# Linear attention with a gated feed-forward block, fp32: the first and the last instructions are rearranged, and the last four tiles of the normalised input are turned by VectorE by way of DRAM

## The chip, the cores and the metric

One core of one Trainium2 chip. The metric is the device time of one launch in microseconds (us). The core's engines run side by side, each with its own queue of instructions in a fixed order: TensorE (PE in the profile, with its weight loads as PEld), VectorE (DVE), ScalarE (ACT) and GpSimd (POOL) compute, SyncE (SP) issues the DMA transfers. They wait for each other by semaphores.

## The reference

```python
x  = A_x                                  # 1 x 2048 x 512
xn = (x - mean(x)) / sqrt(var(x) + 1e-5)  # over the last axis
q, k, v = (xn @ wqkv) split into 32 heads of 16
pq, pk  = phi(q), phi(k)                  # phi(t) = where(t > 0, t + 1, exp(t)) + 1e-6
kv  = einsum("bhsd,bhse->bhde", pk, v);  z = sum of pk over s
o   = einsum("bhqd,bhde->bhqe", pq, kv) / (einsum("bhqd,bhd->bhq", pq, z) + 1e-6)
s   = o @ wo                              # 512 x 512
g   = silu((gelu(xn @ w_gate) * (xn @ w_up)) @ w_down)   # 512 -> 1792 -> 512
out = x + s * g
```

## The kernel before

All data is fp32. TensorE multiplies in a rounded form (fp32r), so each operand is split in a high part (cast by ScalarE, names ending in h) and a low part (a subtraction by VectorE, names ending in l), and a product is three passes: high by high, high by low, low by high (`three`). The large products are done with seven instead of eight block products (Strassen's way), and X, Y, Z, FX, FY, FZ, dX, dY, dZ are the sums in PSUM that gather them.

*Stages.* The 16 tiles of 128 tokens go in eight pairs n = 0 to 7, each pair with tiles i = 0 and 1. For each pair: load x; `ln` makes the statistics on VectorE, rstd on GpSimd and xn on VectorE (L648); `transp` turns a tile of xn with four 128x128 transposes on TensorE into a PSUM bank pt (L696), from which ScalarE copies it to xt in SBUF (L498); `split_x` casts Xh from pt and VectorE subtracts for Xl; `forms` makes the sums T of xt on GpSimd for the block products; then come the products with the weights of k and q (kq), in X, Y and Z. For pairs 2 to 7 these stand on TensorE as X(n), Y(n), Z(n); for the first two (`CL = 2`) as plain sums k and q. From X, Y and Z come q and k, by ScalarE's kr and qr and VectorE's kp and qp; qp is written to DRAM (q_d) and read back later. `split_xn` splits xn itself (xnh, xnl), and the sums gps gather pk by xn, of four 128-row pieces each. So xn of every tile is read by TensorE's transposes and by `split_xn`.

Meanwhile `prep_early` makes three of the gate and up weights' groups of sums (raw is the load, tmp the sums, we the split result) in four groups each, and writes both halves of each group to DRAM (w_d). From about 133 us on come the feed-forward products with Xh, Xl and the weights w (FX, FY, FZ), the attention's own matrices (pkv, pm, M), then the products with w_down (dX, dY, dZ gathered in acc), and the last sums sps = pq by M (`attn`), in four chunks of 512 tokens by four blocks n of 128 columns. Each sps is multiplied into silu(acc) or a stored g by VectorE (L1323), the transposed x (sxr, loaded by DMA) is added (L504), and the result is stored (`out_tile`).

In `turn`, late in the kernel, a tile q is read back from q_d with its rows mixed (each partition gets the rows of one residue), scaled, and turned by one VectorE transpose in squares of 32x32 (L1260).

*What sets the order.* Every instruction is first recorded by `do` with an engine, a cost, the buffers it reads and writes, and for TensorE a key; a planner (`Plan`) then sets the order on each engine. TensorE follows the list `pe_keys`; the other engines follow from how soon the planner needs a result, with `plan.due` as a time set by hand for some. `KEPT` lists draws that altered this order at random within windows of time, one after the other. Buffers belong to pools of numbered units (`U(name, units, ...)` takes the next free one of its list); the next user of a unit waits for the last reader. A bank is one of the eight in PSUM. `R0`, `R1`, `TMP` are units of 4 KB a partition for raw weights.

```python
    def prep_early(q):
        raw, t = sums_w(q, R0)
        for g, src in enumerate(sources(raw, t)):
            n = GROUPS[g].stop - GROUPS[g].start
            v = raw_tile(R1, f"we{q}{g}", [P, 2, D]) if g % 2 else None
            f = [(half(v, hl) if v else tile_in("up", 34 + hl, [P, D], F32, f"we{q}{g}{hl}")).map(
```

So the groups alternate between two places here: units 34 and 35, and R1.

Of the kernel before, what the change touches and what calls it, by code (L numbers as in the profile page):

```python
# [9 lines left out]
F32 = mybir.dt.float32  # L10
# [5 lines left out]
P = 128  # L16
# [3 lines left out]
    (85, 100, [10000006]),  # L20
    (70, 85, [10000048]),
    (-1, 12, [10000061]),
    (40, 55, [10000175]),
    (135, 200, [10000200]),
    (25, 40, [10000230]),
    (40, 55, [10000342]),
    (85, 100, [10000376]),
    (40, 55, [10000415, 10000462]),
    (500, 560, [10000471]),
    (-1, 12, [10000515]),  # L30
    (500, 560, [10000523, 10000590, 10000640]),
    (115, 135, [10000649]),
    (500, 560, [10000723]),
    (115, 135, [10000785]),
    (500, 560, [10000819, 10000833]),
    (340, 420, [10000924]),
    (115, 135, [10000994]),
    (-1, 12, [10001161, 10001223, 10001300]),
    (270, 340, [10001313, 10001357]),
    (-1, 12, [10001377]),  # L40
    (500, 560, [10001410]),
    (-1, 12, [10001492]),
    (40, 55, [10001818]),
    (-1, 12, [10001854]),
    (500, 560, [10001973]),
    (340, 420, [10002732]),
    (135, 200, [10006848]),
    (85, 100, [10010611]),
    (270, 340, [10010753]),
    (40, 55, [10010839]),  # L50
    (340, 420, [10010858]),
    (500, 560, [10010942, 10011053]),
    (40, 55, [10011765]),
    (135, 200, [10011937]),
    (-1, 12, [1010000092]),
    (340, 420, [1010000637, 1010002072]),
    (25, 40, [1010003933]),
    (500, 560, [1010016325, 1010018040]),
    (70, 85, [1010018047, 1010018667, 1010018893, 1010020523]),
    (55, 70, [1010020607]),  # L60
    (85, 100, [1010021997]),
    (100, 115, [1010030646]),
    (115, 135, [1010032131]),
    (100, 115, [1010033698]),
    (500, 560, [1010034750, 1010034866]),
    (135, 200, [1010038225]),
# [10 lines left out]
WARM = 14, 3  # L77
# [318 lines left out]
def kernel(  # L396
# [78 lines left out]
    q_d = dram_view([NT, KT, P, P], "q_d", NT)  # L475
    g_d = dram_view([D, S // 2], "g_d", NT // 2)
# [86 lines left out]
    idle = bank(0, "warm", (P, P))  # L563
    do("PE", 0.427 * 10, warm, idle, ones, key="warm")
# [59 lines left out]
    CL = 2  # L624
    a21 = [[tile_in("up", 15 + 2 * lo + k, [P, D], F32R, f"a21{lo}{k}") for k in range(2)] for lo in range(2)]
# [8 lines left out]
    def ln(*ts):  # L634
        n = len(ts)
        mv = little("mv", f"mv{ts[0]}", [P, n, 2])
        for i, t in enumerate(ts):
# [7 lines left out]
           rstd, ve, neg_half)  # L645
        for i, t in enumerate(ts):
            xns[t] = U("xn", range(4, 9), f"xn{t}")
            do("DVE", 0.46, lambda o, i, m, r: nc.vector.tensor_scalar(o, i, m, r, op0=ALU.subtract, op1=ALU.mult),  # L648
               xns[t], xs.pop(t), mv[:, i, 0:1], rstd[:, i:i + 1], name=f"xn{t}")
# [38 lines left out]

    def transp(n, i):
        t = tokens[n][i]  # L690

        pt = bank(3 + 2 * n + i if 0 < 2 * n + i < 2 * CL else 1, f"pt{t}", (P, KT, P))

        def run(o, a, b):
            for k in range(KT):
                nc.tensor.transpose(o[:, k, :], a[:, k * P:(k + 1) * P], b)  # L696
            if n == 0 and i == 0:
                warm(idle(), ones(), WARM[1])
        do("PE", 0.4, run, pt, xns[t], ident, key=("T", n, i), name="T", more=(idle,) if n == 0 and i == 0 else ())
# [3 lines left out]
        xts[n, i] = v.part((v.res[i],), (slice(None), i))  # L703
        copy("ACT", xts[n, i], pt, D, f"xt{n}{i}")
        pts[n, i] = pt
# [16 lines left out]
    def split_x(n, i):  # L722
        if i == 0 and n == 0:
            for s in range(2):
                split(xrows("h", s, s + 1, [0]), xrows("l", s, s + 1, [0]), pts[0, 0][:, 2 * s:2 * s + 2], 2 * P, "Xa")
# [13 lines left out]
    def split_xn(t):  # L739
        h = U("xnh", range(9, 12), f"xnh{t}", F32R)  # L740
        lo = U("xnl", range(12, 15), f"xnl{t}", F32R)
        copy("ACT", h, xns[t], D, "xnh")
        tt("DVE", "sub", lo, xns[t], h, D, "xnl")
        xn_s[t] = h, lo
# [96 lines left out]
    for n in range(NP):  # L841
        if n == 0:
# [3 lines left out]
        for i in range(2):  # L846
            load_next()
            transp(n, i)
            split_x(n, i)
# [42 lines left out]
    pe_keys.append(("T", 0, 0))  # L892
# [64 lines left out]
    EARLY = range(11, 14)  # L957
# [5 lines left out]

    GT = []
# [287 lines left out]
    def turn(p, t):  # L1252
# [7 lines left out]
        do("DVE", 1.03, lambda o, i: nc.vector.transpose(  # L1260
            o.rearrange("p g (s t) -> p g t s", t=KT), i.rearrange("p (t g d) -> p g t d", t=KT, d=32)),
           v, pn, name="turn", port=False)
# [14 lines left out]
    def attn(c, M, place):  # L1277
# [29 lines left out]
    def out_tile(c, n, ps):  # L1307
# [7 lines left out]
            xr = U("g", SPOTS, f"sxr{c}{n}")  # L1315
# [112 lines left out]
```

## Time and profile before

| | us |
|---|---|
| median of three runs | 604.91 (604.63, 604.91, 607.84) |
| profiled execution, device time | 605.64 |
| its span in the trace | 603.5 |
| TensorE busy | 594.2 (98%) |
| VectorE busy | 517.0 (86%) |
| ScalarE busy | 347.1 (58%) |
| GpSimd busy | 243.0 (40%) |

The mean granted clock of TensorE was 0.997. A row of the timeline has the start and the length in us, the engine and line, the operation, what it writes and reads, the shape and a count; in brackets the time that the engine stood idle just before, and what ended it. Several equal instructions in a row are one row. A matmul's length runs to its modelled end, so a row overlaps with the next: the distance between starts is what a matmul costs. In groups, the three numbers after a count are the smallest, the median and the largest duration in ns. DMA rows have the size of one transfer and the median time from issue to landing.

### The profile page before, as it was taken

The page shows a single profiled execution, that of the slowest core. Times are in us where ns is not written, and L with a number is a line of the kernel's source. Part 1 is how long each engine was busy: PE and PEld are TensorE (multiplying, and loading weights), DVE is VectorE, ACT ScalarE, POOL GpSimd, SP SyncE. Part 2 cuts the span into 40 slices and gives each one's busy share as a digit, 9 for nine tenths or more (in the row PEclk, how much of TensorE's full clock was granted, in tenths as well). Part 3 has the DMA queues.
Part 4 walks back from the last instruction along what each step waited for, and adds up shares of the span by engine and source line. Part 5 has one row for each costly group of instructions (what it writes and reads, how often), then busy time and mean ns, then how long its engine had stood idle before and what let it go on. Part 6 is the DMA issues. An engine that isn't in the chain of part 4 may idle for free.

```text
span 603.5 us, 7883 instructions
## 1 busy us (share of the span) xinstructions
PE 594.2 (98%) x2636; PEld 483.4 (80%) x2636; DVE 517.0 (86%) x819; ACT 347.1 (58%) x627; POOL 243.0 (40%) x237
## 2 busy tenths in 40 slices
PE   9999999999999999999999999999999999999996
PEld 7887877788878888888888777788888888886885
DVE  6999998787689899999899766668899898987995
ACT  6687888787576655655344566655353444445530
POOL 4456757757535372615053830522222130325000
PEclk9999999999999999999999999999999999999998
DMA  7259954779863344667964999744555665568577
GB/s 243 70 154 273 292 187 137 220 212 352 349 232 129 134 175 174 223 225 270 364 213 153 364 394 351 299 164 153 191 193 191 204 215 190 194 202 295 195 252 259
DMA packets 73384, 137.09 MB, mean 227 GB/s; under 512 B 4352, under 2 KB 43264, under 8 KB 69248
## 3 DMA queue, kind: packets, MB, share of 16 engines
q1 hardware_dynamic: 73344, 136.59, 64.8%
q8 instruction: 21, 0.34, 0.2%
q14 instruction: 19, 0.16, 0.1%
HBM read 85.72 MB, written 50.86 MB: 226 GB/s over the span
## 4 chain that ended last, share of the span: by engine, by line
PE 87%; DVE 6%; DMA 4%; ACT 1%; issue 1%; POOL 0%; DVEq 0%; ACTq 0%; POOLq 0%
PE FX L531 24%; PE FZ L531 12%; PE dX L531 11%; PE gps L531 7%; PE FY L531 6%; PE dZ L531 5%; PE X L531 5%; PE dY L531 3%; PE Z L531 2%; PE k L531 2%; PE q L531 2%; PE sps L531 2%; DMA sxr<-in_A_xT 2%; PE Y L531 1%; DMA pql<-t_d 1%
## 5 line engine op out<-in xcount | busy, mean ns | idle before, releaser
L531 PE MATMUL FX<-Xh,w 128*128 128x512 f32 x448 | 135.2, 391 | 0.0
L531 PEld LDWEIGHTS FX<-Xh,w 128*128 128x128 f32 x448 | 83.9, 188 | 18.3 <-ACT fu L498 0.6
L1194 POOL TENSOR_TENSOR h<-h,g 128x512 f32<-128x512 f32 x28 | 41.3, 1475 | 99.5 <-DVE h L504 95.5
L531 PE MATMUL FZ<-Xh,w 128*128 128x512 f32 x224 | 69.8, 393 | 0.0
L531 PE MATMUL FX<-Xl,w 128*128 128x512 f32 x224 | 68.9, 390 | 0.1
L1154 DVE TENSOR_TENSOR acc<-acc,dX 128x512 f32<-128x512 f32 x76 | 51.8, 681 | 19.4 <-PE dX L531 18.9
L498 ACT CAST hfh<-sums 128x512 fp32r<-128x512 f32 x56 | 34.5, 622 | 48.9 <-DVE sums L504 48.4
L498 ACT COPY fu<-FX 128x512 f32<-128x512 f32 x56 | 32.9, 587 | 42.2 <-PE FX L531 40.6
L504 POOL TENSOR_TENSOR tmp<-raw 128x256 f32<-128x256 f32 x28 | 27.4, 992 | 66.9 <-DVE w L504 35.3
L531 PEld LDWEIGHTS FZ<-Xh,w 128*128 128x128 f32 x224 | 42.0, 188 | 9.9 <-issue 1.0
L531 PEld LDWEIGHTS FX<-Xl,w 128*128 128x128 f32 x224 | 42.0, 188 | 9.2 <-ACT fu L498 0.5
L504 DVE TENSOR_TENSOR hfl<-sums,hfh 128x512 fp32r<-128x512 f32 x56 | 42.5, 764 | 4.2 <-ACT hfh L498 3.3
L531 PE MATMUL dX<-hfl,dh 128*128 128x512 f32 x112 | 43.9, 394 | 1.1 <-DVE acc L1154 0.6
L1007 POOL TENSOR_TENSOR qz<-qz,zq 128x512 f32<-128x512 f32 x16 | 23.4, 1465 | 50.9 <-DMA qz<-q_d 44.5
L531 PE MATMUL dX<-hfh,dl 128*128 128x512 f32 x112 | 43.7, 391 | 0.0
L531 PE MATMUL dX<-hfh,dh 128*128 128x512 f32 x112 | 43.7, 392 | 0.0
L504 POOL TENSOR_TENSOR sums<-draw 128x256 f32<-128x256 f32 x28 | 22.0, 795 | 45.0 <-DMA draw<-in_B_w_down 34.3
L1154 DVE TENSOR_TENSOR acc<-acc,dZ 128x512 f32<-128x512 f32 x52 | 35.5, 683 | 3.9 <-PE dZ L531 3.8
L498 ACT CAST hfh<-h 128x512 fp32r<-128x512 f32 x42 | 26.0, 621 | 15.3 <-POOL h L1194 5.4
L531 PE MATMUL FY<-Xh,w 128*128 128x512 f32 x112 | 34.3, 390 | 0.3 <-ACT FY L498 0.3
L531 PE MATMUL FZ<-Xl,w 128*128 128x512 f32 x112 | 34.3, 390 | 0.0
L504 DVE TENSOR_TENSOR hfl<-h,hfh 128x512 fp32r<-128x512 f32 x42 | 32.8, 781 | 0.0
(197 smaller groups left out, 1490.6 us busy)
## 6 DMA issues: line engine op xcount, KB each, us to landing
w<-w_d SPq DMA_DIRECT2D x17, 1792.0 KB, 7.6
w_d<-w SPq DMA_DIRECT2D x11, 1792.0 KB, 8.0
draw<-in_B_w_down SPq DMA_DIRECT2D x14, 512.0 KB, 6.1
w_d<-we SPq DMA_DIRECT2D x18, 256.0 KB, 3.3
x<-in_A_x SPq DMA_DIRECT2D x16, 256.0 KB, 4.0
q_d<-qp SPq DMA_DIRECT2D x16, 256.0 KB, 2.9
qz<-q_d SPq DMA_DIRECT2D x16, 256.0 KB, 4.5
q<-q_d SPq DMA_DIRECT2D x16, 256.0 KB, 3.3
```

The costliest lines, as they stand in the source:

```text
L498: do("ACT", act(n, src.psum), lambda o, i: nc.scalar.copy(o, i), dst, src, name=name)
L504: do(eng, c, lambda o, p, q: getattr(e, f"tensor_{op}")(o, p, q), dst, a, b, name=name)
L531: nc.tensor.matmul(o if r is None else o[:, r], a, b, start=first, stop=made == self.passes[r], skip_group_check=self.on or r is not None)
L1007: do("POOL", pool(D), lambda o, z: nc.gpsimd.tensor_mul(o, o, z.unsqueeze(1).to_broadcast([P, KT, P])), rows_of(q), zq, name="u")
L1154: do("DVE", dve(D), lambda o, i: nc.vector.tensor_add(o, o, i), o, ps, name="acc")
L1194: do("POOL", pool(NC), lambda o, i: nc.gpsimd.tensor_mul(o, o, i), h, g, name="h")
```

## The change

*At the front.* There are 12 and 2 warming matmuls instead of 14 and 3, in another bank. The four transposes of the very first tile go in two halves with their own keys and their own parts of the bank, so that Xh of the first half can be cast when two transposes are done. The order in which SP issues the first loads is another: x of the second tile now stands ahead of the weights wk, and x of the third between them.

*At the end.* The last sum (chunk 1, block n = 3) is two sums of 256 columns in two banks, 24 matmuls of 256 columns instead of 12 of 512, and `out_tile` takes the two. The x loads of the last chunk go to units of their own (`FREED`), which hfh and hfl left, and no longer to the ring of the stored g.

*In the middle.* For n = 6 and 7 (`TX = 6`), xn is made by ScalarE in one activation (scale rstd, bias nb, and VectorE makes nb = -mean * rstd once for the pair), written to DRAM (xn_d), read back with mixed rows into xq in units 34 and 35, and turned by one VectorE transpose straight into xt (`squares`); there are no transposes on TensorE and no copies from PSUM for these four tiles, and Xh and Xl are split from xt. For the rows to fit, the columns of x, the columns of q and the rows of v are put in another order ahead of the launch, and for n below 6 VectorE's xn writes through a view that puts them back. As units 34 and 35 are in use, all groups of `prep_early` go through R1.

The draws of `KEPT` are others as well, so the order differs in many places.

```diff
 KEPT = [
-    (85, 100, [10000006]),
+    (500, 560, [230000001]),
...
-WARM = 14, 3
+WARM = 12, 2
...
-    idle = bank(0, "warm", (P, P))
+    idle = bank(7, "warm", (P, P))
...
+        if ts[0] in [t for p in tokens[TX:] for t in p]:
+            nb = little("nb", f"nb{ts[0]}", [P, n])
+            do("DVE", 0.11, lambda o, i, r: nc.vector.scalar_tensor_tensor(o, i, -1.0, r, op0=ALU.mult, op1=ALU.mult),
+               nb, mv[:, :, 0], rstd)
+            for i, t in enumerate(ts):
+                xns[t] = U("xn", range(4, 9), f"xn{t}")
+                do("ACT", act(D), lambda o, i, r, b: nc.scalar.activation(o, i, AF.Identity, bias=b, scale=r),
+                   xns[t], xs.pop(t), rstd[:, i:i + 1], nb[:, i:i + 1], name=f"xn{t}")
+                rows = xns[t].map(lambda ap: ap.rearrange("p (q e) -> p q e", e=P))
+                dma(xn_d(t, t).map(lambda ap: ap.rearrange("q s e -> s q e")), rows, 256)
+            return
...
+    def squares(dst, src):
+        do("DVE", 1.03, lambda o, i: nc.vector.transpose(
+            o.rearrange("p g (s t) -> p g t s", t=KT), i.rearrange("p (t g d) -> p g t d", t=KT, d=32)),
+           dst, src, name="turn", port=False)
...
+        if n >= TX:
+            s = U("xq", [34, 35], f"xq{t}")
+            dma(s.map(lambda ap: ap.rearrange("p (i e) -> p i e", e=P)),
+                xn_d(t, t).map(lambda ap: ap.rearrange("q (s i) e -> (q s) i e", i=KT)), 256)
+            squares(xts[n, i], s)
+            pts[n, i] = xts[n, i]
+            return
...
-            v = raw_tile(R1, f"we{q}{g}", [P, 2, D]) if g % 2 else None
-            f = [(half(v, hl) if v else tile_in("up", 34 + hl, [P, D], F32, f"we{q}{g}{hl}")).map(
+            v = raw_tile(R1, f"we{q}{g}", [P, 2, D])
+            f = [half(v, hl).map(
...
+    pe_keys[:] = [k for k in pe_keys if k[0] != "T" or k[1] < TX]
...
+            if (c, n) == (CHUNKS[-1], KT - 1):
+                halves = []
+                for m in range(2):
+                    cs = slice(m * NC // 2, (m + 1) * NC // 2)
+                    ps = bank(ring("sps", [3, 4, 2, 0, 1]), f"sps{c}{n}{m}", (P, NC // 2))
+                    Sum(ps).add(("S", c, n, m), *three([[v[:, k, rows] for v in M] for k in range(KT)],
+                                                       [[v[:, cs] for v in f] for f in forms_]), name="S", cost=SHORT)
+                    halves.append(ps)
+                out_tile(c, n, halves)
+                continue
...
-            xr = U("g", SPOTS, f"sxr{c}{n}")
+            xr = U(*(("xr", FREED) if c == CHUNKS[-1] else ("g", SPOTS)), f"sxr{c}{n}")
...
+    FREED = [*FHH, *FHL]
```

Three places of the new order. In the rows a name is that of a buffer with a running number, `<-` stands ahead of what is read, and x2 is a count.

ScalarE, before, at the casts for the first tile of n = 7 (pt_1340; we_1328 and we_1367 are groups of early weights, u and pkh belong to n = 6):

```order
L498 CAST we_1328<-raw_1242 128x512
L498 COPY xt_1347<-pt_1340 128x512
L498 CAST Xh_172<-pt_1340 128x4x128
L498 COPY u_6_1355<-X_1238 128x512
L771 ACTIVATE pkh_1361<-kp_1338 128x512
L498 CAST we_1367<-raw_1242 128x256
L498 COPY xt_1347<-pt_1369 128x512
```

The same place now (xt_1365 is n = 7, X_1233 belongs to n = 6):

```order
L533 CAST we_1326<-tmp_1107 128x512
L533 COPY u_6_1334<-X_1233 128x512
L843 ACTIVATE pkh_1338<-kp_1316 128x512
L533 CAST xnh_1343<-xn_1052 128x512
L832 ACTIVATE qr_1356<-c_6_1345 128x512
L832 ACTIVATE qr_1368<-X_1233 128x512
L833 ACTIVATE qr_1368<-qr_1368 128x512
L833 ACTIVATE qr_1356<-qr_1356 128x512
L533 CAST we_1388<-raw_1229 128x512
L533 CAST Xh_173<-xt_1365 128x4x128
```

Xh of n = 7 now comes from xt, behind u, pkh and qr of n = 6 and behind two groups of early weights that share R1.

SP, now, from the load draw on (xn_1269 and xn_1290 are the two tiles of n = 7, xq_1319 and xq_1354 what is read back):

```order
L529 DMA draw_0_1288<-in_B_w_down 128x2x512
L529 DMA w_d<-we_1263 128x512
L529 DMA xn_d<-xn_1269 128x4x128
L529 DMA w_d<-we_1263 128x512
L529 DMA xn_d<-xn_1290 128x4x128
L529 DMA xq_1319<-xn_d 128x512
L529 DMA w_d<-we_1326 128x512 x2
L529 DMA xq_1354<-xn_d 128x512
L529 DMA wvo_1362<-in_A_wo 128x512
```

Before, the w_d issues alone stood between draw and wvo; now four issues of n = 7 stand among them, and the reads wait for the writes.

TensorE, before, the last rows:

```order
L531 MATMUL sps_5775<-pql,M_5192 128x512 x8
L531 MATMUL sps_5775<-pql,M_5313 128x512 x4
L531 MATMUL sps_5792<-pql,M_5192 128x512 x8
L531 MATMUL sps_5792<-pql,M_5313 128x512 x4
```

And now:

```order
L566 MATMUL sps_5763<-pql,M_5180 128x512 x8
L566 MATMUL sps_5763<-pql,M_5317 128x512 x4
L566 MATMUL sps_5780<-pql,M_5180 128x256 x8
L566 MATMUL sps_5780<-pql,M_5317 128x256 x4
L566 MATMUL sps_5795<-pql,M_5180 128x256 x8
L566 MATMUL sps_5795<-pql,M_5317 128x256 x4
```

The last sum is two of half the width, one after the other, in banks of their own.

More of the change, by code (lines that the diff above doesn't have):

```diff
@@ L37 @@
[L37 to L53, printed above, removed]
@@ L561, in warm @@
             nc.tensor.matmul(o, w, w, start=True, stop=True)
-    idle = bank(0, "warm", (P, P))
-    do("PE", 0.427 * 10, warm, idle, ones, key="warm")
+    idle = bank(7, "warm", (P, P))
+    do("PE", 0.427 * 11.5, warm, idle, ones, key="warm")
     pe_keys.append("warm")
@@ L687 @@
     xts, Ts, pts = {}, {}, {}
+    def squares(dst, src):
+        do("DVE", 1.03, lambda o, i: nc.vector.transpose(
+            o.rearrange("p g (s t) -> p g t s", t=KT), i.rearrange("p (t g d) -> p g t d", t=KT, d=32)),
+           dst, src, name="turn", port=False)
     def transp(n, i):
         t = tokens[n][i]
[L692 to L699, printed above, removed]
         if i == 0:
@@ L841 @@
     for n in range(NP):
+        if n >= TX and XDUE:
+            plan.due = 15.6 * n - XDUE
         if n == 0:
```

165 lines of the change are left out of this document (123 added, 42 removed).

## The prediction

> **What bounds the kernel now.** I read the page's busy shares and its chain of waits first, then a table of windows, then the timeline of the places that the change touches.
>
> ```profile
> PE 594.2 (98%) x2636; PEld 483.4 (80%) x2636; DVE 517.0 (86%) x819; ACT 347.1 (58%) x627; POOL 243.0 (40%) x237
> PE 87%; DVE 6%; DMA 4%; ACT 1%; issue 1%; POOL 0%; DVEq 0%; ACTq 0%; POOLq 0%
> 70.00:84.00 14.00, 14.00 (x66) 11.23 (x65) 13.80 (x24) 10.73 (x20) 8.21 (x8) 1.00 0.71 216
> 84.00:100.00 16.00, 16.00 (x75) 12.93 (x75) 14.43 (x25) 12.77 (x25) 11.01 (x11) 1.00 0.54 182
> 100.00:115.00 15.00, 15.00 (x70) 11.91 (x69) 11.91 (x20) 11.86 (x23) 11.19 (x11) 1.00 0.72 219
> 115.00:135.00 20.00, 19.64 (x89) 15.85 (x88) 17.52 (x25) 16.06 (x31) 11.53 (x11) 1.00 0.66 200
> ```
>
> TensorE is busy for 594.2 of the span's 603.5 us, and the chain is its matmuls for 87%. In the windows (length, then PE, PEld, DVE, ACT, POOL, granted clock, DMA share, GB/s), where the moved work sits, it has no gap but 0.36 us. So whatever leaves its queue there shortens the run one for one, until something that it reads comes late. VectorE is the next: 0.20 us idle of 14 at 70 to 84, then 1.57, 3.09 and 2.48, together 7.14 us from 84 to 135.
>
> **The change part by part.** Times are for the profiled execution, 605.64 us, which is 0.73 above the median of 604.91; I subtract that at the end.
>
> *The sixteen transposes.* The timeline of TensorE around the first four of the last pair (n=7):
>
> ```profile
> 111.48 0.62 PE L531 MATMUL X<-kq,Xl 128*128 128x512 f32 x2
> 111.94 0.60 PE L696 MATMUL pt<-ident,xn 128*128 128x128 f32 x4
> 112.30 0.71 PE L531 MATMUL gps<-pkh,xnh 128*128 128x512 f32 x2
> 112.85 0.63 PE L531 MATMUL gps<-pkl,xnh 128*128 128x512 f32 x2
> ```
>
> Two wide matmuls take 0.46 from start to start (111.48 to 111.94), so 0.23 each. From 111.94 to 112.85 are 0.91 us for four transposes and two wide ones: the four cost 0.91 - 0.46 = 0.45. Four such groups go: **-1.8 us**, all on the path. The Trainium skill (VectorE: DVE Perf Modes, The three transpose paths) gives 390 ns for a TensorE transpose of 128x128; by that the sixteen would be worth 6.2 us and the sum would be 4.4 lower. The measured 0.11 us each, pipelined, decides.
>
> *What VectorE and ScalarE get for it.* The turn has the same form as one that the kernel does later:
>
> ```profile
> L1260 DVE STREAM_TRANSPOSE sums<-q x16: 1081/1094/1118, 252.5 to 534.8; 128x512 f32<-128x512 f32 x16
> L648 DVE TENSOR_SCALAR xn<-x,mv,rstd x16: 531/538/1520, 5.3 to 107.0; 128x512 f32<-128x512 f32 x16
> L498 ACT COPY xt<-pt x16: 567/588/618, 10.8 to 115.4; 128x512 f32<-128x512 f32 x16
> L760 ACT ACTIVATE kr<-c 128x512 f32<-128x512 f32 x6 | 3.8, 633 | 2.0 <-DVE qp L763 1.5 <-DVE c L504 0.3
> ```
>
> VectorE: four turns of 1.09 and two tiny nb (at most 0.15 each) less four xn of 0.54, +2.5 us, against 7.14 idle: covered, if it falls where the idle time is. ScalarE: four xn at 0.63 or a little over for four copies at 0.59, no change. Nothing of this is on the path by itself.
>
> *The way through DRAM, and the one buffer.* This is the doubtful term. A tile of n=7 is now written to DRAM, read back and turned before Xh and Xl can be cast, and four DMA issues stand in SP's queue for each pair, with the weights' w_d issues, the wo loads and q_d behind them. SP waits at each read for its write's landing. And each group of early weights (we) must have both halves in DRAM before ScalarE casts the next group, as units 34 and 35 now hold xq.
>
> ```profile
> q_d<-qp SPq DMA_DIRECT2D x1, 256.0 KB, 2.5
> w_d<-we SPq DMA_DIRECT2D x17, 256.0 KB, 3.8
> draw<-in_B_w_down SPq DMA_DIRECT2D x1, 512.0 KB, 5.7
> w_d<-we SPq DMA_DIRECT2D x3, 256.0 KB, 6.0
> q<-q_d SPq DMA_DIRECT2D x16, 256.0 KB, 3.3
> 119.15 0.73 PE L531 MATMUL X<-kq,Xl 128*128 128x512 f32 x2 [0.35 <-DVE qp L763]
> ```
>
> The issues: a write of this size alone at 26 us took 2.5 us to land; seventeen between 78 and 150 us had a median of 3.8; three behind the draw load (issued 106 to 107) took 6.0. The same size read back took 3.3. When is the tile needed? X of n=7 starts at 119.15 - 0.35 = 118.8 without its wait. In the new order five wide matmuls more and sixteen transposes fewer stand ahead of it, and the front comes 0.4 earlier (below): 118.8 + 1.15 - 1.8 - 0.4 = 117.75. ScalarE's new order has, in this sequence: we of one group, u, pkh, qr, we of the next, then Xh of n=7. The group before these two is ready where its like is now:
>
> ```profile
> 107.00 0.53 DVE L648 TENSOR_SCALAR xn<-x,mv,rstd 128x512 f32<-128x512 f32 x1
> 103.35 0.62 ACT L498 CAST we<-tmp 128x512 fp32r<-128x512 f32 x1
> 106.40 0.68 DVE L504 TENSOR_TENSOR we<-tmp,we 128x512 fp32r<-128x512 f32 x1
> 104.00 0.33 SPq L494 DMA_DIRECT2D w_d<-we  x1
> ```
>
> Its second half is written by 107.1, its w_d issued by 107.5, a microsecond behind the draw. From there: a landing, a cast of 0.62, VectorE's half of 0.68 and an issue of 0.33 (1.6 together), a second landing, then the next we cast and Xh, 0.6 each. With 3.8 twice Xh is there at 107.5 + 3.8 + 1.6 + 3.8 + 1.2 = 117.9, with 6.0 twice at 122.3: 0.15 to 4.55 us late. The round trip itself (xn_d issued near 107, as the last xn is now; 3.8 to 6.0; xq 3.3; turn 1.09; Xh 0.6) gives 115.8 to 118.0, so the one buffer comes later. I take 4.9 for the first landing, midway between the rows, as it starts right behind the draw, and 3.8 for the second, which has nothing so large ahead: 119.0, 1.25 late. As the old 0.35 at X goes, **+0.9** net (-0.2 to +4.2). For n=6 no draw is ahead, and its turns stand near 95 with the first use near 101: **+0.2** (0 to +1). The Trainium skill (DMA: Bandwidth & Descriptors, Anatomy of one DMA, written for those that GpSimd issues) has a fit of 2.0 us plus bytes at 436 GB/s, an estimate of 2.6 for 256 KB; by that nothing would be late and the sum 1.5 lower. The lone 2.5 us agrees with it, the 6.0 behind the draw does not.
>
> *The front.*
>
> ```profile
> 1.12 5.82 PE L561 MATMUL warm<-ones 128*128 128x128 f32 x28 [1.12 <-DVE neg_half L552]
> 4.45 0.15 DVE L642 TENSOR_SCALAR ve<-mv 128x1 f32<-128x1 f32 x1
> 5.28 0.55 DVE L648 TENSOR_SCALAR xn<-x,mv,rstd 128x512 f32<-128x512 f32 x1 [0.67 <-POOL rstd L644]
> 6.55 0.69 DVE L639 BATCH_NORM_STATS2 st<-x 128x6 f32<-128x512 f32 x1
> 6.77 0.60 PE L696 MATMUL pt<-ident,xn 128*128 128x128 f32 x4
> 7.28 0.18 DVE L640 BATCH_NORM_AGGREGATE mv<-st 128x2 f32<-128x6 f32 x1
> 8.14 1.17 PE L531 MATMUL k<-kq,Xh 128*128 128x512 f32 x4
> 9.29 1.75 POOL L504 TENSOR_TENSOR kq<-wk,kq 128x512 fp32r<-128x512 f32 x1 [1.00 <-ACT kq L498]
> 11.10 0.19 PEld L531 LDWEIGHTS k<-kq,Xh 128*128 128x128 f32 x1 [0.39 <-POOL kq L504]
> ```
>
> The first transposes start at 6.77, when the 28 warming records end, though xn is ready at 5.83. Four records fewer are 0.4 to 0.8 us; VectorE will do the second tile's statistics ahead of that xn (0.69 + 0.18, from 4.60, where ve ends), which ends at 6.0 then: T near 6.35, -0.4. Two half transposes and fewer warming matmuls would let k start about 0.9 earlier than 8.14. But the k that reads POOL's last kq waits for it at 11.10 already, and its wk load is now one place further back, behind another 256 KB of x. Two more matmuls stand ahead of it (worth 0.45). So between +0.3, if that load is 0.8 late, and -0.9: **-0.4**.
>
> *The end.*
>
> ```profile
> 586.96 11.04 PE L531 MATMUL sps<-pql,M 128*128 128x512 f32 x48
> 595.79 0.69 DVE L504 TENSOR_TENSOR acc<-acc,sxr 128x512 f32<-128x512 f32 x1 [2.65 <-DMA sxr<-in_A_xT]
> 599.05 0.74 DVE L1323 TENSOR_TENSOR acc<-acc,sps 128x256 f32<-128x256 f32 x2
> 599.72 0.75 DVE L504 TENSOR_TENSOR acc<-acc,sxr 128x256 f32<-128x256 f32 x2
> out_yT<-acc SPq DMA_DIRECT2D x2, 128.0 KB, 2.0
> ```
>
> TensorE ends at 598.0, VectorE's last add at 600.47, 2.47 later, since it stood 2.65 us for an x load and then had a queue. With those loads in units that are free earlier, only a product and a sum of the last half follow TensorE: 0.37 + 0.38, with 0.1 to 0.3 for handing over, 0.85 to 1.05 in all. That is -1.4 to -1.6. The last sum is now 24 narrower matmuls, each with its own weights; at the transposes' 0.11 they take as long as 12 wide ones, at 0.14 they take 0.6 more. **-1.4** (-0.8 to -1.6). The landing of 2.0 stays.
>
> *The redrawn order elsewhere* moves instructions everywhere: 0, from -1 to +1, as TensorE's share leaves only 9.3 us of the span outside its work, most of it at the two ends.
>
> Sum: -1.8 + 0.9 + 0.2 - 0.4 - 1.4 = -2.5; 605.64 - 2.5 = 603.1, and 0.73 less for a median: **602.4 us**. A difference of 0.5%, 3.0 us, is about what a measurement of this kernel can tell from none; faster begins below 601.9. With all bounds at one end the forecast would run from 599.4 to 608.8; its likely part is 600.5 to 604.8.
>
> **The rivals.**
> 1. *VectorE becomes the bound* where the turns stand, as idle time is not where they are. For: 0.20 idle of 14 us just ahead, and at n=7 a turn stands in front of the qp that frees the X bank, for which X waited at 119.15. Against: 2.48 idle in that window. Price: two turns in full, 2.2: 604.6. The Trainium skill (VectorE: DVE Perf Modes, Rules for kernel authors) sends a 128x128 transpose to TensorE; that would be its reason here. Chance 0.10.
> 2. *The one buffer chains* (the other side). From near 105 to 131 five groups follow each other, each needing cast, half, issue and landing: 1.6 us and 3.8 make 5.4, or 27 us for five, about what the order leaves. From landings of 4.0 on each adds its excess, and ScalarE's casts for X and kr stand behind them: at 5.5 five times 1.7 = 8.5 late; less the 0.9 that the forecast has and some 1.4 for a group of half the bytes, +6.2: 608.6. For: the 6.0 row. Against: the median of 3.8. Chance 0.17.
> 3. *All fits*: landings near 3.3, so that nothing at n=7 or n=6 is late (-1.3 against the forecast), a front at its best (-0.5) and 0.6 from the redrawn order: 600.0. Chance 0.09.
> 4. *The end does not do what it should*: x still comes late, -1.4 is lost: 603.8. Chance 0.05.
>
> **How the numbers follow.** The forecast has 0.59: 0.26 of it below 601.9, 0.33 within the bound. With rival 3, faster is 0.35; with 1 and 4, same is 0.48; rival 2 is slower, 0.17. From 599.8 to 607.5 leaves out rival 2 and some 0.03 of rival 3.
>
> **What would show it.** No pt group after 100 us, and the distance between gps rows 0.45 shorter; a wait of ScalarE's we cast for w_d's landing, with X of n=7 behind it by 1 to 2 us; T at 6.35 and k's wait for POOL's kq near 11; the last add within 1.1 us of TensorE's end. I am wrong if TensorE's idle time between 84 and 135 exceeds 3 us (then rival 1 or 2, by the releaser: VectorE's turn or a landing), or if the last landing follows TensorE's end by over 4.5.

## The result and the profile after

The changed kernel took 605.82 us (median of 22 runs, 604.38 to 608.61) against 604.95 us for the kernel before (22 runs): a ratio of 1.0013, 95% interval 1.0002 to 1.0025. It is slower by about 0.8 us, clear of no change by that interval, but less than the 0.5% (3.0 us) that the prediction took as what can be told, where 2.5 us less was forecast. The profiled execution took 606.09 us with a span of 604.4.

The page's busy shares and chain of the changed kernel, and the last three of the four windows that were shown of before (length, then PE, PEld, DVE, ACT, POOL, granted clock, DMA share, GB/s):

```profile
PE 594.1 (98%) x2626; PEld 480.3 (79%) x2626; DVE 518.3 (86%) x821; ACT 347.5 (57%) x627; POOL 240.0 (40%) x237
PE 83%; DVE 7%; DMA 4%; ACT 3%; issue 1%; POOL 1%; SPq 0%; DVEq 0%; POOLq 0%; ACTq 0%
84.00:100.00 16.00, 15.18 (x66) 11.89 (x65) 15.46 (x25) 13.38 (x25) 11.86 (x12) 1.00 0.62 198
100.00:115.00 15.00, 13.91 (x62) 11.10 (x61) 10.89 (x19) 11.45 (x21) 5.11 (x5) 1.00 0.74 210
115.00:135.00 20.00, 20.00 (x86) 15.78 (x86) 16.68 (x24) 16.06 (x31) 11.17 (x11) 1.00 0.58 186
```

TensorE was without a gap from 84 to 115 before; now it stands 0.82 and 1.09 us there, and the chain is TensorE's for 83% and no longer 87%. From 100 to 115 VectorE and GpSimd do less as well (10.89 and 5.11 us, against 11.91 and 11.19). The timeline of TensorE at four of its waits after 80 us, and of what it waited for (two others, 0.41 at 555 and 0.39 at 158, are larger than the one at 88; the kernel before has one like the first, 0.48 at 553):

```profile
85.11 0.73 PE L566 MATMUL gps<-pkl,xnh 128*128 128x512 f32 x2 [0.54 <-DVE pkl L844]
87.73 1.21 PE L566 MATMUL X<-kq,Xh 128*128 128x512 f32 x4 [0.28 <-DVE qp L835]
114.81 1.20 PE L566 MATMUL X<-kq,Xh 128*128 128x512 f32 x4 [1.09 <-ACT u L533]
580.17 0.50 PE L566 MATMUL dX<-hfh,dh 128*128 128x512 f32 x1 [0.67 <-DVE acc L1232]
...
81.97 1.69 DVE L814 TENSOR_TENSOR xnl<-xn,xnh 128x512 fp32r<-128x512 f32 x1
84.40 0.66 DVE L844 SCALAR_TENSOR_TENSOR pkl<-kp,pkh 128x512 fp32r<-128x512 f32 x1
85.16 0.81 ACT L689 ACTIVATE xn<-x,nb,rstd 128x512 f32<-128x512 f32 x1 [0.25 <-DVE nb L685]
85.89 0.62 ACT L833 ACTIVATE qr<-qr 128x512 f32<-128x512 f32 x1
113.66 0.62 ACT L533 CAST we<-tmp 128x512 fp32r<-128x512 f32 x1 [2.54 <-DMA w_d<-we]
114.18 0.58 ACT L533 COPY u<-X 128x512 f32<-128x512 f32 x1
578.83 0.69 DVE L1411 TENSOR_TENSOR g<-g,sps 128x512 f32<-128x512 f32 x1 [1.26 <-DMA g<-g_d]
579.43 0.68 DVE L1232 TENSOR_TENSOR acc<-acc,dX 128x512 f32<-128x512 f32 x1
```

Each wait is one queue's order. At 85, pkl stands behind an xnl of 1.69 us and two statistics. At 88, qp waits for its qr, which stands behind ScalarE's new xn of 0.81 us. At 114, the we cast waits 2.54 us for the landing of w_d (the one buffer), and u, which frees X's bank, stands behind it. At 580, acc stands behind a g whose load is late; the prediction had not looked there.

To compare whole kernels I add up how far TensorE falls behind its own work: the start of a matmul less the work that stood ahead of it (0.227 us for 512 columns, half of that for 256, 0.109 for a transpose; warming left out). The table is that lag's growth in each stretch, in us, from one profile each; "work" is the sum of all work ahead of the last matmul, and "last" is when that starts.

| kernel | order | to 20 | 20-80 | 80-90 | 90-122 | 122-200 | 200-540 | 540-600 | work | last |
|---|---|---|---|---|---|---|---|---|---|---|
| before | old | 8.71 | 1.32 | 0.20 | 1.18 | 0.29 | 3.11 | 2.81 | 580.00 | 597.62 |
| changed | new | 8.77 | 0.95 | 1.98 | 1.43 | 2.79 | 2.48 | 3.64 | 578.37 | 600.43 |
| two_buffers | new | 7.96 | 1.38 | 1.65 | 0.35 | 2.52 | 2.50 | 4.63 | 578.37 | 599.35 |
| mended | new | 8.82 | 1.02 | 1.09 | 1.16 | 2.52 | 2.53 | 3.36 | 578.37 | 598.86 |
| middle_undone_2 | new | 8.23 | 1.23 | 1.60 | 0.35 | 2.75 | 2.71 | 3.56 | 580.12 | 600.58 |
| no_zacc | new | 8.55 | 1.01 | 0.97 | 1.84 | 1.97 | 2.46 | 4.20 | 578.37 | 599.36 |
| end_only | old | 9.57 | 1.32 | 0.22 | 1.18 | 0.28 | 3.06 | 1.76 | 580.12 | 597.51 |
| both_ends | old | 9.47 | 1.32 | 0.19 | 1.16 | 0.21 | 2.70 | 1.80 | 580.12 | 596.98 |
| no_transposes | old | 9.25 | 1.30 | 0.94 | 2.80 | 0.84 | 3.28 | 1.79 | 578.25 | 598.45 |
| no_transposes_2 | old | 9.06 | 1.32 | 0.11 | 2.64 | 0.25 | 3.11 | 2.07 | 578.25 | 596.82 |
| old_order | old | 9.27 | 1.32 | 1.83 | 2.78 | 1.28 | 2.67 | 2.37 | 578.37 | 599.89 |

From before to changed the work falls by 1.63 us and the lag grows by 4.42 (1.78 at 80 to 90, 0.25 to 122, 2.50 to 200, 0.83 after 540, less 0.94 elsewhere), so the last matmul starts 2.81 later; the span after that start shrinks by 1.9 (603.5 - 597.62 = 5.9, now 604.4 - 600.43 = 4.0). That is the span's +0.9.

### The profile page after: what moved, and what is told of

It reads as the page before. It is cut to its first block, busy times and chain, and to the rows that moved or that the text cites. A ratio compares the mean times of both kernels' runs of the same rounds, so it can differ in the third digit from the quotient of the medians.

```text
span 604.4 us, 7866 instructions
## 1 busy us (share of the span) xinstructions
PE 594.1 (98%) x2626; PEld 480.3 (79%) x2626; DVE 518.3 (86%) x821; ACT 347.5 (57%) x627; POOL 240.0 (40%) x237
## 4 chain that ended last, share of the span: by engine, by line
PE 83%; DVE 7%; DMA 4%; ACT 3%; issue 1%; POOL 1%; SPq 0%; DVEq 0%; POOLq 0%; ACTq 0%
PE FX L566 22%; PE FZ L566 11%; PE dX L566 11%; PE FY L566 6%; PE gps L566 6%; PE dZ L566 6%; PE X L566 5%; PE sps L566 5%; PE dY L566 3%; PE Z L566 2%; PE k L566 2%; PE q L566 2%; DVE sums L539 1%; PE Y L566 1%; DMA pql<-t_d 1%; DVE hfl L539 1%
## 5 line engine op out<-in xcount | busy, mean ns | idle before, releaser
L1272 POOL TENSOR_TENSOR h<-h,g 128x512 f32<-128x512 f32 x28 | 40.7, 1453 | 113.8 <-DVE h L539 113.7
L539 POOL TENSOR_TENSOR tmp<-raw 128x256 f32<-128x256 f32 x28 | 24.7, 888 | 69.5 <-DVE w L539 50.0
L539 DVE TENSOR_TENSOR hfl<-sums,hfh 128x512 fp32r<-128x512 f32 x56 | 40.5, 733 | 3.5 <-ACT hfh L533 2.6
L539 POOL TENSOR_TENSOR sums<-draw 128x256 f32<-128x256 f32 x28 | 24.6, 885 | 38.6 <-DMA draw<-in_B_w_down 38.6
L539 DVE TENSOR_TENSOR hfl<-h,hfh 128x512 fp32r<-128x512 f32 x42 | 35.1, 840 | 1.8 <-ACT hfh L533 1.8
```

The source lines that it names most:

```text
L539: do(eng, c, lambda o, p, q: getattr(e, f"tensor_{op}")(o, p, q), dst, a, b, name=name)
L1272: do("POOL", pool(NC), lambda o, i: nc.gpsimd.tensor_mul(o, o, i), h, g, name="h")
```

## The experiments

All ratios are to the kernel before, run beside them on the same chip, in five rounds. An edit "of the order" changes nothing but the position of the named instructions; the rest of that kernel's order is written out and stays. Theory A: the transposes are worth what they take, and single new waits eat it. Theory B: VectorE paces the middle, so that time saved comes back at its next late result. C and D came later, from the first results.

**two_buffers.** The changed kernel in its own order, with two buffers for we again, in units that x has left:

```diff
-            v = raw_tile(R1, f"we{q}{g}", [P, 2, D])
-            f = [half(v, hl).map(
+            v = raw_tile(R1, f"we{q}{g}", [P, 2, D]) if g % 2 or q == EARLY[0] else None
+            f = [(half(v, hl) if v else tile_in("up", hl, [P, D], F32, f"we{q}{g}{hl}")).map(
```

> The changed kernel with its order of instructions kept word for word; only, groups of early weights w_d of the second and third quarter alternate between R1 and two units that held x and are free from 87 us on. Theory A (one buffer: ScalarE's we cast waits 2.54 us for w_d's landing at 113.66, so u and X of n=6 at 114.81 wait 1.25): that wait of ScalarE goes, X of n=6 waits under 0.2, and the time falls by 1.0 to 1.4 us, to 0.9977 to 0.9983 of the changed kernel, 0.999 to 1.000 of before. Rival B (TensorE's saved time comes back at the next wait, whatever it is; here Xh of n=7, behind the turn that ends at 117.4): X of n=7 waits 1 us instead, and the time falls by under 0.3.

Measured: 604.36 us, 0.9991 (0.9977 to 1.0004), 0.9978 of the changed kernel. The wait of 1.25 us at 114 is gone (lag from 90 to 122: 0.35 and not 1.43). So the one buffer cost 1.1 us where it stood, 1.3 (plus or minus 1.1) by the times, as theory A had it: it does not chain. But the profile has 1.0 us more lag after 540 (4.63 and not 3.64), where a sum now waits 0.58 us at 583 for a late g, so the trace doesn't show that the whole of it stays won.

**end_only.** The old order, with the change at the end alone (the last sum in two halves, the last x loads in units of their own).

```diff
-            xr = U("g", SPOTS, f"sxr{c}{n}")
+            xr = U(*(("xr", FREED) if c == CHUNKS[-1] else ("g", SPOTS)), f"sxr{c}{n}")
...
+            if (c, n) == (CHUNKS[-1], KT - 1):
+                halves = []
```

> Before, with its order kept, and only the end changed: the last sum in two halves of 256 columns, the x loads of the last chunk in units that hfh and hfl left, issued some 5 us earlier. Theory A: only the tail shortens; the last add ends 0.9 us after TensorE instead of 2.5, the sum itself costs 0.1 to 0.3 more, so -1.3 to -1.6 us (0.9974 to 0.9979), and the 0.83 us wait of dX at 580 of the changed kernel is not here, as it comes of the redrawn order. Rival B (the earlier x loads slow the g loads, so VectorE's products with g come late and dX waits): a wait of 0.5 to 1 at about 580, and -0.4 or less.

Measured: 604.03 us, 0.9983 (0.9972 to 0.9994). VectorE's last rows in it:

```profile
597.83 0.42 DVE L1333 TENSOR_TENSOR acc<-acc,sps 128x256 f32<-128x256 f32 x1 [0.17 <-PE sps L531]
598.28 0.42 DVE L504 TENSOR_TENSOR acc<-acc,sxr 128x256 f32<-128x256 f32 x1
```

The last add ends at 598.70, 1.2 us after the start of TensorE's last matmul (597.51), and waits for no load any more.

**front_only.** The old order, with the warming of 12 and 2, the other bank and the first transposes in two halves.

```diff
-WARM = 14, 3
+WARM = 12, 2
...
-            pe_keys.append(("T", 0, 0))
+            pe_keys += [("T", 0, 0, 0), ("T", 0, 0, 1)]
```

> Before, with its order kept, and at the front only 12 and 2 warming matmuls and the first four transposes in two halves; the loads are issued in the order of before. Theory A (the last wk load and GpSimd's kq set the pace: k waits for it at 11.10): T starts 0.4 to 0.8 earlier, k too, and waits as much longer for kq: 0 to -0.2 us. Rival B (my prediction's term): -0.4 or more. If fewer warming matmuls leave the first k at the slow clock, up to +0.5.

Measured: 604.63 us, 0.9991 (0.9978 to 1.0004): not told from nothing. The lag at 20 us scatters by 0.9 between profiles of kernels whose front is the same, so that one profile can't weigh it either.

**no_transposes.** The old order, with the sixteen transposes and their four copies left out:

```diff
+        if n >= 6:
+            dma(xts[n, i], ext(x[t * P:(t + 1) * P, :].rearrange("p (k c) -> p k c", c=P)), 256)
...
+            return
```

> Before, with its order kept, without the last sixteen transposes and their four copies from PSUM; xt of n=6 and 7 is loaded by DMA from x some 8 us ahead instead, so Xh and Xl there hold rows of x that are not turned, and the output is not the reference's. Everything else (xn on VectorE, two places for early weights) is before's. Theory A (TensorE has no other limit there): -1.5 to -1.9 us (0.997). Rival B (VectorE's qp and ScalarE's u set the pace of X, so that the waits at 119 and after grow): -0.6 or less.

Measured: 606.06 us, 1.0013 (0.9996 to 1.0030): with 1.75 us of work less, no gain. One row of TensorE, the rows of VectorE ahead of it, and GpSimd beside them:

```profile
105.48 0.73 PE L531 MATMUL X<-kq,Xh 128*128 128x512 f32 x2 [2.33 <-DVE qp L771]
...
98.86 1.58 DVE L504 TENSOR_TENSOR Xl<-xt,Xh 128x512 fp32r<-128x512 f32 x1
100.37 1.22 DVE L780 SCALAR_TENSOR_TENSOR pkl<-kp,pkh 128x512 fp32r<-128x512 f32 x1
101.52 1.23 DVE L504 TENSOR_TENSOR xnl<-xn,xnh 128x512 fp32r<-128x512 f32 x1
102.67 1.22 DVE L504 TENSOR_TENSOR we<-raw,we 128x512 fp32r<-128x512 f32 x1
104.75 0.68 DVE L771 SCALAR_TENSOR_TENSOR qp<-X,qr 128x512 f32<-128x512 f32 x1
...
99.85 1.20 POOL L504 TENSOR_TENSOR T<-xt 128x256 f32<-128x256 f32 x1
```

And the same place in the kernel before:

```profile
98.07 0.68 DVE L504 TENSOR_TENSOR Xl<-pt,Xh 128x512 fp32r<-128x512 f32 x1
99.70 0.68 DVE L504 TENSOR_TENSOR xnl<-xn,xnh 128x512 fp32r<-128x512 f32 x1
100.30 0.68 DVE L504 TENSOR_TENSOR we<-raw,we 128x512 fp32r<-128x512 f32 x1
101.94 0.69 DVE L763 SCALAR_TENSOR_TENSOR qp<-X,qr 128x512 f32<-128x512 f32 x1
100.55 1.02 POOL L504 TENSOR_TENSOR T<-xt 128x256 f32<-128x256 f32 x1 [1.33 <-ACT xt L498]
```

GpSimd's T starts 0.7 earlier than there, and now falls on xnl and we, which took 0.68 each and take 1.2 here. The Xl ahead of them takes 0.9 more: there it reads pt in PSUM, here xt in SBUF, and GpSimd's zacc (96.78 to 99.90) is beside it. The pkl between took 1.10 there already. So qp starts 2.8 us later than there: some 2.1 by these operations, and 0.8 that the queue was behind at 98 (c at 98.26 and not at 97.47). This speaks for B, with the reserve that the Xl is part of this edit, and not of the transposes' absence alone.

**no_transposes_2.** The same, with qp ahead of we at 105 and ahead of an xnl at 87; an edit of the order.

> As the kernel with the last 16 transposes left out (xn of those tiles replaced by rows of x, so its output is not the reference's; 606.06 us, 1.0013), with VectorE's two qp moved ahead of what stood in front of them: at 87 ahead of one xnl of 1.22 us, at 105 ahead of the we of 1.22 us. TensorE waited 0.49 and 2.33 us for these two. Theory A, the transposes' 1.8 us are there to be had once no wait eats them: 606.06 - 2.3 - 0.5 = 603.3 us, 0.997 (0.9955 to 0.9985) of the kernel before. Theory B, VectorE paces the stage: the next operation in its queue comes late instead, a new wait of 1 us or more for VectorE stands between 87 and 125 us, and the time stays within 0.5 us of 605.

Measured: 604.34 us, 0.9991 (0.9981 to 1.0001): 1.3 us better than without the move, where A said 2.8, and B no more than a new wait. The wait at 87 is gone, that at 105 fell from 2.33 to 0.28, and another grew from 0.31 to 1.11:

```profile
121.64 1.20 PE L531 MATMUL Y<-kq,Xh 128*128 128x512 f32 x4 [1.11 <-ACT Y L498]
119.45 0.62 ACT L498 CAST Xh<-T 128x512 fp32r<-128x512 f32 x1 [1.32 <-POOL T L504]
```

Half of what was put in reach came back 16 us later, and not through VectorE: ScalarE's Y stands behind an Xh that waits 1.32 us for GpSimd's T. Neither theory alone has it.

**mended.** two_buffers with one edit of the order at each wait left: qr and qp ahead of the new xn, pkl ahead of the statistics, acc ahead of the late g, one x load behind two of g.

> The kernel with two we buffers (604.36 us, 0.9991 of the kernel before), with four more edits of the order alone, one at each wait that TensorE still has there: ScalarE's two xn (0.82 and 0.80 us) stand behind the two qr of 0.62 us and VectorE's qp directly behind nb (X waited 0.54 us at 87); VectorE's pkl stands ahead of the statistics of 0.68 and 0.18 us (gps waited 0.69 us at 84); VectorE's acc of dX stands ahead of the g that waits for its landing (dX waited 0.70 us at 578), and one load of xT stands behind two of g_d (sps waited 0.74 us at 583). Theory A, each wait is a price of its own that the changed order added: 602.2 us, 0.9953 of before (0.994 to 0.997). Theory B, VectorE's work paces these stretches and the time saved at one wait comes back at the next: 604 us, 0.998 to 0.9995.

Measured: 604.63 us, 0.9985 (0.9973 to 0.9996). Three of the four waits went; the fourth, of a sum for a late g, is still 0.48 at 582 (0.58 in two_buffers). From 80 to 90 us 0.56 of lag is gone, from 540 on 1.27. But at 89 there is a new wait of 0.25 for ScalarE's Y, and at 103 a larger one:

```profile
103.05 1.19 PE L566 MATMUL X<-kq,Xh 128*128 128x512 f32 x4 [0.53 <-DVE qp L835]
```

What was won from 80 to 90 is lost again before 122 (0.35 became 1.16), as B says for the middle; what was won at 580 stays, as A says.

**both_ends.** end_only and front_only together on the old order.

> The two ends of the change alone, front and end together, on the kernel before's order written out; transposes and we buffers as before. End alone gave 0.9983, front alone 0.9991 (unresolved). If the two add: 0.9974, 603.4 us (0.996 to 0.9985). If the front gives nothing: 0.9983, 603.9 us. Theories A and B expect the same of it, since neither end touches the middle; it says what the change would have been worth without its middle and without the redrawn order.

Measured: 603.22 us, 0.9972 (0.9962 to 0.9983). It has the lowest ratio of this study: the two ends without the middle and without the redrawn order.

**middle_undone** and **middle_undone_2.** The changed kernel in its own order, with the middle undone:

```diff
-    TX = 6
+    TX = 8
...
-            v = raw_tile(R1, f"we{q}{g}", [P, 2, D])
+            v = raw_tile(R1, f"we{q}{g}", [P, 2, D]) if g % 2 else None
```

> The changed kernel in its own order, with the middle alone undone: the last four tiles turned by TensorE again, their xn made by VectorE, and the early w piece's even groups in their two own buffers again. Both ends and the redrawn order stay. Theory A, the middle took back about what it saved (wait for we 1.25 us, xn ahead of qr 0.44 us, against 1.8 us of transposes): 605.8 us, the same as the changed kernel (0.998 to 1.002 of it). Theory B, the transposes moved away were worth their 1.8 us and the loss came from the redrawn order: 607.5 us, 1.003 of the changed kernel.

Measured: 607.74 us, 1.0047 (1.0034 to 1.0059). It can't be read: VectorE's two xn, put where ScalarE's had been, made X wait 1.58 us at 89, and a transpose stood too close behind what frees its bank. The second version puts these three instructions elsewhere.

> As the kernel with the middle alone undone in the changed kernel's order (607.74 us, 1.0047), which had two waits of its own making: VectorE's two xn stood ahead of qp (X waited 1.58 us at 89, against 0.44 in the changed kernel), and a transpose stood close behind the Xl that frees its bank (0.67 us at 117). Here qp stands ahead of the xn and that transpose three matmuls later. If the middle took back what it saved: 606.0 us, 1.0018 of before and 1.0005 of the changed kernel. If the transposes moved away keep their 1.8 us: 607.5 us, 1.003 of the changed kernel.

Measured: 606.32 us, 1.0024 (1.0013 to 1.0034). The changed kernel is 0.9989 of that, 0.7 us (plus or minus 1.0): the middle took back most of what it saved. And this kernel is both ends on the new order, as both_ends is on the old: 1.0052 (plus or minus 0.0015) between them, 3.1 us, for the order, and for where the undone middle's instructions were put by hand. Two of its waits, both of which the changed kernel has too (its largest, 0.81 at 584, is for a late g, near the changed kernel's wait at 580):

```profile
84.59 0.72 PE L566 MATMUL gps<-pkl,xnh 128*128 128x512 f32 x2 [0.53 <-DVE pkl L844]
158.17 0.73 PE L566 MATMUL FX<-Xh,w 128*128 128x512 f32 x2 [0.39 <-ACT fu L533]
```

**old_order.** From here theory C: the redrawn order ate the gain. The whole change on the old order, with its new instructions put by hand into gaps of the queues, two we buffers, and the rows read back into one spare tile (nb has one tile for both pairs, too):

```diff
-            s = U("xq", [34, 35], f"xq{t}")
+            s = U("xq", [36], f"xq{t}")
```

> The whole change (both ends, the last four tiles turned by VectorE via DRAM, their xn on ScalarE) but on the order of the kernel before, written out, with the change's few new operations put into gaps of its queues, and with the two we buffers kept: the rows that come back from DRAM use one other tile instead of those two. It differs from the kernel with two we buffers (0.9991 of before) only in the order and that tile. Theory C, new since the last runs: the redrawn order is what ate the gain (TensorE's start fell back by 1.9 us between 122 and 200 us and by 1.1 us at 580, in every kernel with that order and in none with the old one): 601.8 us, 0.9948 of before (0.993 to 0.9965), and no such waits. Theory B, VectorE paces the middle, so that the transposes' 1.8 us come back as waits for VectorE between 87 and 125 us on this order too, as they did when they were left out: 603.2 us, as both ends alone (0.9965 to 0.9985).

Measured: 606.97 us, 1.0042 (1.0028 to 1.0056), 1.0070 of both_ends. Both numbers that had been given are wrong; the middle costs 4.2 us on this order instead of saving 1.75. TensorE's largest waits, and three of VectorE's rows ahead of them:

```profile
88.49 1.20 PE L566 MATMUL X<-kq,Xh 128*128 128x512 f32 x4 [1.44 <-DVE qp L835]
119.63 1.19 PE L566 MATMUL Z<-kq,Xh 128*128 128x512 f32 x4 [0.81 <-DVE c L539]
122.21 0.74 PE L566 MATMUL X<-kq,Xl 128*128 128x512 f32 x2 [0.72 <-DVE qp L835]
...
83.20 2.10 DVE L539 TENSOR_TENSOR we<-raw,we 128x512 fp32r<-128x512 f32 x2
115.04 1.38 DVE L539 TENSOR_TENSOR Xl<-xt,Xh 128x512 fp32r<-128x512 f32 x1 [0.69 <-ACT Xh L533]
117.95 1.10 DVE L741 STREAM_TRANSPOSE xt<-xq 128x512 f32<-128x512 f32 x1 [0.39 <-DMA xq<-xn_d]
```

Each is VectorE late: at 117.95 the turn waits for its landing and then holds the queue for 1.1 us, with c, pkl and qp behind it. At 115 Xl, which the change makes read xt in SBUF and no longer pt in PSUM, takes 1.38 us. The three such Xl of over 0.9 us here take 1.6 us more than in the changed kernel, where they keep 0.68 (0.41 for half a tile). From 126 us on the lag is the old order's again, 0.2 up to 330. So C is half right: the waits from 122 to 200 belong to the new order. But that order was also what made room for the middle: from 90 to 122 two_buffers, which has as many buffers, loses 0.35, and this kernel 2.78. One placement by hand doesn't show that none would do.

**no_zacc** and **before_no_zacc.** Theory D: VectorE's queue is late because GpSimd stretches it. Both kernels, in their orders, without GpSimd's sixteen sums for zacc:

```diff
-        do("POOL", pool(D), lambda o, i: nc.gpsimd.tensor_add(o, o, i), zacc, p0, name="zacc")
```

> The changed kernel in its own order, with GpSimd's 16 sums zacc<-zacc,kp (1.3 to 1.7 us each, all between 20 and 140 us) left out, so its output is not the reference's; nothing else moves. GpSimd is on no chain there, but VectorE's operations from SBUF to SBUF take 0.68 us alone and up to 1.7 us beside GpSimd. Theory D, new since the last runs: VectorE's queue, stretched so, is what makes pkl (0.71 us at 85), qp (0.44 us at 88) and kp (0.35 us at 139) late, and what ate the middle: VectorE's stretched operations go back to 0.68 us and these waits go; 604.2 us, 0.9987 of before (0.997 to 1.000), a larger fall than the kernel before has from the same cut. Theory A, the waits come from the order and the landings alone: 605.5 us, 1.0008, a fall of at most 0.5 us in both kernels.

> The kernel before in its own order with the same 16 sums of GpSimd left out; its output is not the reference's. Theory D: VectorE is as full (14.8 of 15 us at 70 to 85) but nothing waits for it save one qp (0.52 us at 119), so the fall is smaller than the changed kernel's: 604.5 us, 0.9992 (0.998 to 1.000). Theory A: the same fall as in the changed kernel, at most 0.5 us.

Measured: 604.10 us, 0.9989 (0.9978 to 1.0000), and 603.87 us, 0.9984 (0.9972 to 0.9995): 1.45 us less in the changed kernel, 1.0 less in the kernel before. The difference of the two falls is inside the intervals, so the times don't decide for D. The trace does for the first wait:

```profile
81.81 0.68 DVE L814 TENSOR_TENSOR xnl<-xn,xnh 128x512 fp32r<-128x512 f32 x1
83.23 0.66 DVE L844 SCALAR_TENSOR_TENSOR pkl<-kp,pkh 128x512 fp32r<-128x512 f32 x1
84.23 0.62 PE L566 MATMUL gps<-pkl,xnh 128*128 128x512 f32 x2
```

The xnl that took 1.69 us takes 0.68, pkl is there at 83.9 and no longer at 85.1, and TensorE doesn't wait. The lag from 80 to 90 falls from 1.98 to 0.97. The wait for the one we buffer stays (1.37 us at 113.8).

## Why the prediction was wrong, step by step

**The redrawn order, counted 0 (-1 to +1): the step that failed.** It cost 3.1 us (both ends on the new order against both ends on the old). The argument was that TensorE's work leaves only 9.3 us of the span, most of it at the two ends. That bounds what an order can gain. It says nothing on what a new one can lose, and the new one loses at 80 to 90 (1.4 us more in the undone kernel than in both_ends), from 122 to 200 (2.5) and after 540 (1.8), and wins 0.8 from 90 to 122. The changed kernel has the losses from 122 to 200 and after 540 as well (2.79 and 3.64, against 0.29 and 2.81 before), so they come neither of the middle, which middle_undone_2 doesn't have, nor of its undoing by hand. The 3.1 us are the order's price without the middle; with it the sign turns: two_buffers is 3.1 us (plus or minus 1.2) faster than old_order. In both pairs the slower kernel is the one whose instructions were put by hand into an order drawn for other code. What is shown is that the term is not 0, and that it hangs on the code; a price for any redrawing isn't shown. The difference of order could be read before the run, place by place; the prediction read it at three places and took the rest as a mean.

**The sixteen transposes, -1.8:** right as work (580.00 to 578.37, with 0.12 added at the end). That it is all on the path until something comes late was right too. What was missing is how soon something is: with the transposes simply left out, 2.3 us came back as one wait for qp. And one cost had no term at all: one of Xl's two inputs moves from PSUM to SBUF, which cost nothing in the changed kernel's order and 1.6 us of VectorE in old_order.

**The middle's waits, +0.9 and +0.2.** The one buffer: right in kind and nearly in size. The sign that was named came in part: the we cast waited 2.54 us for w_d, an X behind it 1.25, and Xh of n=7 was done at 119.3 where 119.0 was worked out. But the X that waited, at 114.81, can't be one of n=7, whose Xh was cast at 118.70: it waited for u of n=6, earlier in the same queue, and after it TensorE didn't wait again before 139, so not for Xh of n=7 either. That its 1.25 us equal the 1.25 that were worked out for n=7 is luck. These rows are an xn_d's issue and the read back, whose wait for landing kept SP from 110.1 to 113.0:

```profile
109.34 0.76 SPq L529 DMA_DIRECT2D xn_d<-xn  x1
112.97 0.33 SPq L529 DMA_DIRECT2D xq<-xn_d  x1
116.29 1.10 DVE L741 STREAM_TRANSPOSE xt<-xq 128x512 f32<-128x512 f32 x1
118.70 0.61 ACT L533 CAST Xh<-xt 128x512 fp32r<-128x512 f32 x1
```

At n=6 the round trip hid, but the xn there did not: counted at 0.63 us "or a little over" from an activation of another form, it took 0.81 and stood ahead of qr (0.44 us at X). Net, the middle was forecast at -0.7 and came to -0.7 (plus or minus 1.0) on the new order, where so close an agreement is luck, and to +4.2 on the old.

**The turns, 1.09:** right, 1.099 by the groups. "Covered, if it falls where the idle time is" was the right condition, and where the order leaves no such place (old_order) it cost 4.2 us. So rival 1, VectorE as the bound where the turns stand (604.6 at a chance of 0.10), is what happens in old_order, though its price of two turns was not what it costs: the price is the queue behind them. In the changed kernel none of the waits shown stands behind a turn. Rival 2, that the one buffer chains, is refuted.

**The front, -0.4.** T started at 5.93 where 6.35 was said. But k waited at its start already, and not for POOL's kq near 11:

```profile
5.93 0.66 PE L767 MATMUL pt<-ident,xn 128*128 128x128 f32 x4 [0.17 <-DVE ve L679]
6.66 1.31 ACT L533 CAST kq<-wk 128x512 fp32r<-128x512 f32 x2 [4.27 <-DMA wk<-in_A_wqkv]
7.87 0.64 ACT L533 CAST Xh<-pt 128x256 fp32r<-128x256 f32 x2
8.29 0.77 PE L566 MATMUL k<-kq,Xh 128*128 128x512 f32 x2 [1.25 <-ACT Xh L533]
```

The wk that the change loads later holds ScalarE's kq casts until 6.66, and Xh stands behind them. By 20 us the lag is 8.77 against 8.71. Here one pair of profiles misleads: five profiles of kernels with the old front show 8.71 to 9.87 (mean 9.29), three with the new front on the old order 9.27 to 9.47, six with the new order 7.96 to 8.82 (mean 8.52). By these the front gives nothing by itself, and the new order's first rows 0.8, which the 3.1 above has in it.

**The end, -1.4:** right. In the changed kernel the last add ends 0.9 us after TensorE, inside the 1.1 that was said:

```profile
597.79 2.92 PE L566 MATMUL sps<-pql,M 128*128 128x256 f32 x23
600.75 0.42 DVE L1409 TENSOR_TENSOR acc<-acc,sps 128x256 f32<-128x256 f32 x1 [0.56 <-PE sps L566]
601.20 0.42 DVE L539 TENSOR_TENSOR acc<-acc,sxr 128x256 f32<-128x256 f32 x1
```

It is -1.9 in the span after the last start. end_only measured -1.0 us, with -1.4 inside its interval, and both ends together -1.7 (0.9972), against the -1.8 of their two terms. In the changed kernel the wait at 580 takes 0.8 of it back.

So the sum was -1.8 for the ends and -0.7 for the middle, both inside what was measured, and 0 for the order, where 3.1 belonged: -2.5 + 3.1 = +0.6, against the +0.8 that was measured. This closing of the sum is no further proof: the three measured parts are ratios of neighbours in one row of four kernels (before, both_ends, middle_undone_2, changed), so they add up to the whole whatever they are. That the new order was the price of the middle's gain, and not an accident beside it, is suggested by old_order and not shown: another order may hold the middle at no loss. The sign against the forecast that was named, over 3 us of idle time for TensorE from 84 to 135, didn't come (1.9); more than half of the losses (from 122 to 200 and after 540) lay outside the stretch that was watched.

## What to carry to other kernels

When a planner's order is drawn anew, the draw is a term of its own, here 3.1 us to one side or the other by the code under it: compare the orders engine by engine over the whole span, and undo the code in the new order, or the order under the new code, before the code gets the credit or the blame. Work taken from a full TensorE is worth its length only up to the next result that another queue has just in time; look for the instruction that is ready last, and ask what stands ahead of it in its queue and how long that takes beside its neighbours. An operation moved to an engine with idle time costs what is queued behind it at its place, not its own length.

## What the runs showed that was not expected

VectorE's operations with two inputs in SBUF take 0.68 us alone, and up to 1.7 us where they fall on GpSimd's work (xnl at 82: 1.69 with zacc beside it, 0.68 without). An Xl that reads one input from PSUM kept 0.69 and the turn its 1.10. The Trainium skill (SBUF — State Buffer, Who interferes with whom) says that a VectorE instruction with two SBUF inputs contends with a GpSimd instruction that reads SBUF, and that one with at most one SBUF input does not, outside VectorE's 2-port modes; the trace agrees in the first, and in the second for the Xl and the turn. It does not settle the second for xn, which has one SBUF tensor as input and in the kernel before took 1.52 us beside a zacc at 47.7 and 0.54 alone: no run here shows which mode it runs in. The consequence here is that an operation's place beside GpSimd, and whether its input lies in PSUM or in SBUF, moved a result of VectorE by 2 us: T 0.7 us earlier and Xl reading xt made qp that much later when the transposes were left out.
